# Low parts of ten weight slices: subtracted on GpSimd instead of VectorE

## The chip, the cores and the metric

The kernel runs on one core of a Trainium2 chip. The metric is the device time of one execution in microseconds (us), as the median of several runs. A core has TensorE (PE in the rows: matrix products), VectorE (DVE) and ScalarE (ACT) for work along rows, GpSimd (POOL) for the same kind of work, and SyncE (SP), which here issues all transfers. Each engine takes its instructions in the order in which they stand in its own queue; waits between engines are semaphores.

## The reference

```python
def _attn_ref(q, k, v, s):                 # q, k, v: (4, 8, 576, 64)
    scores = scale * np.matmul(q, k.transpose(0, 1, 3, 2))
    cum = np.cumsum(np.maximum(s, 0.0), axis=-1)
    bias = -(cum[:, :, :, None] - cum[:, :, None, :])
    scores = np.where(causal, -1000000000.0, scores + np.minimum(bias, 0.0))
    ...
    return np.matmul(attn, v)              # softmax over the last axis

def _moe_ref(x, w_in, w_out):              # first expert: 2304 x 512 -> 2048 -> 512
    h = x @ w_in
    g = h - np.tanh(h)
    return g @ w_out

def _moe2_ref(x, w_in, w_out):             # second expert, the same sizes
    h = x @ w_in
    g = h * np.clip(h + 3.0, 0.0, 6.0) / 6.0
    return g @ w_out
```

The attention's output is the first expert's input, and that expert's output is the second's. The weights of both experts come as 64-bit floats.

## The kernel before

**The three stages.** Attention runs to 185 us, the first expert from there to about 578 us, the second to the end. A matrix product is made to more than the engine's own precision by splitting both sides into a high part (rounded) and a low part (what is left), and by three passes: high by high, low weights by high, high weights by low.

**The first expert** goes through the 2304 tokens in five blocks, and in each block through 16 *slices* of 128 hidden features, numbered 0 to 15. A *step* is one slice of one block:

- three passes of 4 matmuls into a bank (`h{block}_{slice}_0` to `_2`, L903): high weights by high tokens, low weights by high tokens, high weights by low tokens. The first pass needs the slice's high weights, the second its low ones;
- on ScalarE tanh of the bank (L914), on VectorE bank minus tanh (L918), on ScalarE the high part of the result (L922), and its low part (L924), on VectorE in the first three blocks and on GpSimd in the last two. All four use one buffer, `g`, so the next step's tanh waits for L924;
- three passes of 4 matmuls for the output (`o{block}_{slice}_0` to `_2`, L934).

**The weights of a slice** are converted once, on the way into block 0, and stay in SBUF as `w{slice}` (128 partitions x 2048, high and low, for both matrices). Slices 0 to 5 are converted half by half (512 columns) during attention. Slices 6 to 15 (the diff's `range(6, 16)`) are converted whole (1024 columns) while block 0 already runs: one transfer of the raw words (L821), the absolute value on ScalarE (L825), four integer and clamp steps on VectorE (L826, L828, L830, L832) that make a 32-bit float from the two raw words, the high part on ScalarE (L851), and the low part as a subtraction (L852). The float stands in a work buffer from L825 to the end of L852: `wy` and `wy_b` take turns, and late in the block `wy_c` is there as well.

**Who sets the order.** The kernel does not write its instructions in a fixed order. Every piece is entered as an operation with an engine, a duration, what it comes after, its buffers and a priority. `Plan.schedule` then plays the whole program through with these durations and writes each engine's queue in the order of the planned starts. An operation entered with `port=True` is not planned beside another of that kind; the conversion's steps on VectorE are entered so. Durations given to the plan decide the order alone, and the chip takes what it takes.

After the first expert's weights VectorE and ScalarE convert those of the second (L987, L1017, L1018), which go out to HBM and come back as pieces in the last stage.

Of the kernel before, what the change touches and what calls it, by code (L numbers as in the profile page):

```python
# [66 lines left out]
]  # L67
UMX = ((0, 1, 2, 3, 4, 5), (4, 0, 1, 3, 2))
KDMA = ()
TINY, HUGE = (float(np.array([b], np.uint32).view(np.float32)[0]) for b in (0x38000000, 0x47F00000))  # L70

BLOCKS = [(0, t0, w) for t0, w in ((0, 512), (512, 512), (1024, 256), (1280, 512), (1792, 512))]
# [182 lines left out]
def vec_us(n, ghz, fixed):  # L255
    return (n / ghz + fixed) / 1e3
# [3 lines left out]
def kernel(  # L260
# [10 lines left out]
    nc = tc.nc  # L271
    plan = Plan()
    ctx.enter_context(tc.manual_schedule())

    def f32(a):
        return a.bitcast(F32)
# [39 lines left out]
    def r(b):  # L316
        return late[b.t] if isinstance(b.t, str) else b.t
# [132 lines left out]
    def heads(p):  # L450
# [10 lines left out]
        for i, a in enumerate(parts):  # L461
# [33 lines left out]
            oq1.append(plan.op("ACT", act + 0.22 * (p > 0), q1, [lq, al], [b1, tq], early(t + PRIO["q1"], 1), name=f"q1_{p}"))  # L495
            if p in KDMA:
                okh.append(plan.op("ACT", act, lambda a=a: nc.scalar.activation(r(b1)[1][0:64, a, 0:S], r(tq)[64:128, a], AF.Copy), [lk, al], [b1, tq], t + PRIO["kh"], name=f"kh{p}"))
# [314 lines left out]
    def rounded(src, n, prio, after, raws, words, name):  # L812

        raw, y = Buf(raws), Buf(words)

        def word(i):
            return r(raw).rearrange("p (n t) -> p n t", t=2)[:, :, i]

        def load():
            dst = r(raw) if src.ndim == 2 else r(raw).rearrange("p (l m) -> p l m", l=2)  # L820
            nc.sync.dma_start(dst, src)  # L821

        one, two, act = vec_us(n * 512, 1.92, 150), vec_us(n * 512, 0.96, 155), vec_us(n * 512, 1.2, 195)
        ld = plan.dma(load, 512 * n, after, [raw], prio, name=name)
        a = plan.op("ACT", act + 0.05, lambda: nc.scalar.activation(f32(r(y)), f32(word(1)), AF.Abs), [ld], [raw, y], prio)  # L825
        b = plan.op("DVE", one, lambda: nc.vector.tensor_scalar(  # L826
            f32(r(y)), f32(r(y)), TINY, HUGE, op0=ALU.max, op1=ALU.min), [a], [y], prio, port=True)
        b = plan.op("DVE", one, lambda: nc.vector.tensor_scalar(  # L828
            r(y), r(y), 3, 0x3FFFFFF8, op0=ALU.logical_shift_left, op1=ALU.bitwise_and), [b], [y], prio, port=True)
        b = plan.op("DVE", two, lambda: nc.vector.scalar_tensor_tensor(  # L830
            out=r(y), in0=word(1), scalar=-0x40000000, in1=r(y), op0=ALU.bitwise_and, op1=ALU.bitwise_or), [b], [raw, y], prio, port=True)
        b = plan.op("DVE", two, lambda: nc.vector.scalar_tensor_tensor(  # L832
            out=r(y), in0=word(0), scalar=29, in1=r(y), op0=ALU.logical_shift_right, op1=ALU.bitwise_or), [b], [raw, y], prio, port=True)
        return y, b

    def convert(fc, parts, prio, after, raws, words, there=()):
        n = len(parts)
        src = w1[fc][:, parts[0] * 512 : (parts[-1] + 1) * 512].bitcast(I32)
        y, b = rounded(src, n, prio, after, raws, words, f"wl{fc}_{parts[0]}")

        def hi():
            return slots[fc][:, parts[0] : parts[-1] + 1, 0:512]

        def lo():
            return slots[fc][:, parts[0] : parts[-1] + 1, 512:1024]

        def flat():
            return f32(r(y)).rearrange("p (i n) -> p i n", i=n)

        two, act = vec_us(n * 512, 0.96, 155), vec_us(n * 512, 1.2, 195)  # L850
        c = plan.op("ACT", act, lambda: nc.scalar.activation(hi(), flat(), AF.Copy), [b, *there], [y], prio)  # L851
        d = plan.op("DVE", two, lambda: nc.vector.tensor_sub(lo(), flat(), f32(hi())), [c], [y], prio, name=f"wd{fc}_{parts[0]}", port=True)  # L852
        return c, d

    wready, early, first_late, last_slots = {}, [], [], close
    for fc in range(NW):
        for part in range(2):
            wready[fc, part] = convert(
                fc, [part], PRIO["conv"] + 2 * fc + part, [st_done[1][0]], rawp, wyp)
            early += wready[fc, part]  # L860
    to_gg = change(early, "gg", [P, 4, 512], F32R, "B", None, ["gh0", "gh1", "gl0", "gl1"])
    plan.op("V", 0.0, lambda: None, early, hook=lambda: wywp.free.append(wy_t[:, 0:2].rearrange("p i n -> p (i n)")))
    for fc in range(NW, NFC):
        if fc == NFC - 2:
            last_slots = plan.op("V", 0.0, lambda: [slot_alloc(spaces[0], i, f"W{i}") for i in (NFC - 2, NFC - 1)], first_late, prio=0)
        beside = fc in LATE_D
        done = convert(fc, [0, 1], 5000 + 2 * fc, [st_done[20][0]], rdp if beside else rp, wywp, [last_slots])
        wready[fc, 0] = wready[fc, 1] = done
        first_late += done if beside else []
# [565 lines left out]
```

## Time and profile before

| | us |
|---|---|
| runs | 948.28, 948.75, 952.16 (median 948.75) |
| the profiled execution's own time | 947.19 |
| its span (first to last instruction) | 945.4 |
| TensorE busy | 931.6 |
| VectorE busy | 662.9 |
| ScalarE busy | 467.7 |
| GpSimd busy | 159.2 |

The profile is of one execution. The 1.8 us between its span and its own time lie around the program. An engine's busy time is a sum over the whole span; which engine is waited for in a stage is read from the idle time of the others in that stage. The granted clock of TensorE was 0.999 over the span (of its level of 2.4 GHz).

### The profile page before, as it was taken

What the parts mean: (1) busy time and instruction counts of PE and PEld (TensorE: products, weight loads), DVE (VectorE), ACT (ScalarE), POOL (GpSimd) and SP (SyncE); (2) the same over time, 40 slices, a digit from 0 to 9 for tenths busy, and PEclk for the clock granted to TensorE, in tenths of its full rate; (3) what the DMA queues carried; (4) which work ended last, traced back from release to release, by engine and by line L of the source; (5) the groups of instructions that cost most, each with busy time, mean ns of one, the idle gap of its engine ahead of it and who ended that gap; (6) DMA issues with size and microseconds to landing.
All of it is one profiled execution on the core that took longest, in us unless ns stands there. A gap on an engine that the chain in (4) does not pass through costs nothing.

```text
span 945.4 us, 18016 instructions
## 1 busy us (share of the span) xinstructions
PE 931.6 (99%) x7124; PEld 839.5 (89%) x7124; DVE 662.9 (70%) x1059; ACT 467.7 (49%) x720; POOL 159.2 (17%) x113
## 2 busy tenths in 40 slices
PE   8999999999999999999999999999999999999998
PEld 5888888788788889988888888999999999999997
DVE  7898887699985776676577641847767477674853
ACT  7678777555443444444344333544445445454441
POOL 7446656400000000022332321000000000000000
PEclk9999999999999999999999999999999999999999
DMA  5757785977235455563546862767887778776772
GB/s 142 185 153 204 200 227 144 247 308 218 96 121 223 179 183 218 200 202 156 219 149 224 262 215 85 258 214 221 274 268 242 215 226 270 269 245 209 220 217 89
DMA packets 69792, 193.74 MB, mean 205 GB/s; under 512 B 11856, under 2 KB 20656, under 8 KB 68428
## 3 DMA queue, kind: packets, MB, share of 16 engines
q1 hardware_dynamic: 69708, 192.59, 64.0%
q8 instruction: 56, 0.92, 0.4%
q14 instruction: 28, 0.23, 0.1%
HBM read 143.74 MB, written 44.09 MB: 199 GB/s over the span
## 4 chain that ended last, share of the span: by engine, by line
PE 88%; DVE 5%; DMA 3%; SPq 1%; issue 1%; ACT 1%; POOL 0%; DVEq 0%; POOLq 0%; ACTq 0%
PE bank L903 19%; PE pair L1271 19%; PE pair L1195 18%; PE bank L934 18%; PE bank L633 6%; PE bank L666 4%; PE bank L677 2%; PE bank L531 2%; PE wide L531 1%; DMA tq<-in_q_dram 1%; DMA raw_a<-in_w_dram 1%; SPq L735 1%; DMA w<-wdram 1%; DMA rb<-rdram 1%; DVE gg L924 0%
## 5 line engine op out<-in xcount | busy, mean ns | idle before, releaser
L934 PE MATMUL bank<-gg,w 128*128 128x512 f32 (+1 forms) x960 | 233.0, 368 | 1.4 <-ACT gg L922 1.4
L903 PE MATMUL bank<-xx,w 128*128 128x512 f32 (+1 forms) x960 | 232.4, 368 | 0.1
L934 PEld LDWEIGHTS bank<-gg,w 128*128 128x128 f32 x960 | 170.4, 188 | 31.5 <-ACT gg L922 1.8
L903 PEld LDWEIGHTS bank<-xx,w 128*128 128x128 f32 x960 | 170.3, 189 | 30.7 <-DVE xx L887 0.8
L1195 PE MATMUL pair<-op_w,w 128*128 128x384 f32 x648 | 118.0, 335 | 0.2 <-DVE g L918 0.2
L1195 PEld LDWEIGHTS pair<-op_w,w 128*128 128x128 f32 x648 | 112.4, 188 | 1.2 <-DVE g L918 0.6
L914 ACT ACTIVATE g<-bank 128x512 f32<-128x512 f32 (+1 forms) x80 | 44.5, 556 | 129.2 <-PE bank L903 57.3
L924 POOL TENSOR_TENSOR gg<-g,gg 128x512 fp32r<-128x512 f32 x32 | 48.0, 1501 | 345.4 <-ACT gg L922 248.2
L918 DVE TENSOR_TENSOR g<-bank,g 128x512 f32<-128x512 f32 (+1 forms) x80 | 50.8, 634 | 69.9 <-ACT g L914 68.9
L1271 PE MATMUL pair<-w,op_W 128*128 128x256 f32 x774 | 97.9, 283 | 1.2 <-DMA w<-wdram 1.2
L1271 PEld LDWEIGHTS pair<-w,op_W 128*128 128x128 f32 x774 | 95.4, 192 | 1.4 <-DMA w<-wdram 1.4
L922 ACT ACTIVATE gg<-g 128x512 fp32r<-128x512 f32 (+1 forms) x80 | 47.0, 588 | 51.3 <-DVE g L918 27.2
L633 PE MATMUL bank<-Q,K 128*128 128x320 f32 (+9 forms) x384 | 65.2, 309 | 0.4 <-DMA Q<-mdram 0.4
L636 ACT ACTIVATE pt<-bank 128x512 f32<-128x512 f32 (+2 forms) x128 | 58.9, 507 | 11.9 <-PE bank L633 9.9
L1271 PE MATMUL pair<-w,op_B 128*128 128x256 f32 x486 | 62.7, 283 | 0.0
L633 PEld LDWEIGHTS bank<-Q,K 128*128 128x128 f32 (+3 forms) x384 | 56.3, 184 | 5.5 <-issue 1.6
L1271 PEld LDWEIGHTS pair<-w,op_B 128*128 128x128 f32 x486 | 60.5, 192 | 0.0
L540 DVE CUSTOM_DVE_ANT_0 xr<-bank,xr 128x512 bf16<-128x512 f32 (+3 forms) x96 | 48.7, 508 | 15.3 <-PE bank L531 8.8
L474 POOL TENSOR_TENSOR Q<-tq,Q 64x1152 fp32r<-64x1152 f32 (+1 forms) x17 | 43.0, 2531 | 44.7 <-DVE xr L576 18.4
L666 PE MATMUL bank<-pt,vf 128*32 128x192 f32 (+3 forms) x1152 | 47.5, 316 | 1.3 <-ACT pt L636 1.3
L484 POOL TENSOR_TENSOR K<-tq,K 64x1152 fp32r<-64x1152 f32 (+1 forms) x17 | 42.9, 2525 | 9.6 <-ACT pt L636 5.2
L666 PEld LDWEIGHTS bank<-pt,vf 128*32 128x32 f32 x1152 | 32.4, 110 | 12.5 <-ACT pt L636 2.3
(322 smaller groups left out, 1349.7 us busy)
## 6 DMA issues: line engine op xcount, KB each, us to landing
w<-wdram SPq DMA_DIRECT2D x149, 512.0 KB
wdram<-cv SPq DMA_DIRECT2D x56, 512.0 KB
raw_c<-in_w_dram SPq DMA_DIRECT2D x11, 1024.0 KB
raw_b<-in_w_dram SPq DMA_DIRECT2D x11, 1024.0 KB
raw_a<-in_w_dram SPq DMA_DIRECT2D x12, 512.0 KB
vf<-in_v_dram SPq DMA_DIRECT2D x16, 330.0 KB
rb<-rdram SPq DMA_DIRECT2D x32, 144.0 KB
xdram<-xb SPq DMA_DIRECT2D x16, 288.0 KB
```

What stands on the lines that cost most here:

```text
L540: nc.vector.tensor_tensor_reduce(out=junk[0:rr, 0:w], in0=r(b)[0:rr, col : col + w], in1=maskB[:, 0:w] if hh < 0 else maskA[0:rr, m0 : m0 ...
L633: nc.tensor.matmul(o, w, x, start=(i == 0), stop=(i == len(mms) - 1), skip_group_check=True)
L636: nc.scalar.activation(r(pt), r(b)[:, 0 : CW[c]], AF.Exp, scale=0.125)
L666: nc.tensor.matmul(r((wide_b, rest_b)[far])[32 * i : 32 * i + 32, oc : oc + n], r(vf)[:, j, hh, d0 : d0 + 32], r(pts[hh][c])[:, col : col ...
L903: nc.tensor.matmul(r(ps)[:, 0:w], wt[:, c, :], x(c)[:, 0:w], start=(part == 0 and c == 0), stop=(part == 2 and c == NCC - 1),)
L914: nc.scalar.activation(r(g)[:, 0:w], r(ps)[:, 0:w], AF.Tanh)
L918: nc.vector.tensor_sub(x, r(ps)[:, 0:w], x)
L922: gho = plan.op("ACT", vec_us(w, 1.2, 205), lambda: nc.scalar.activation(r(gh)[:, 0:w], r(g)[:, 0:w], AF.Copy), [m, to_gg], [g, gh], base)
L924: glo = plan.op("DVE" if beside else "POOL", vec_us(w, 0.96, 155) if beside else vec_us(w, 0.44, 160), lambda: (nc.vector if beside else n ...
L934: nc.tensor.matmul(r(acc[e])[:, 0:w], a[:, es], bb[:, 0:w], start=f, stop=l)
L1195: nc.tensor.matmul(bank(k)[:, l], w[hw][:, l, kc], r(x)[:, hx, kc], start=(i in (1, 5, 2) and j == 0 and kc == 0), stop=(j == 2 and kc == ...
L1271: nc.tensor.matmul(r(c[k])[:, m * 256 : (m + 1) * 256], r(x)[:, hx, l, m * P : (m + 1) * P], w[hw][:, l], start=(i == order[chain_first[k] ...
```

## The change

For slices 6 to 15 the subtraction that makes the low part is entered as an operation of GpSimd, without `port=True`, and with a planned duration for GpSimd. Nothing else is edited.

```diff
+LO_POOL = range(6, 16)
...
         c = plan.op("ACT", act, lambda: nc.scalar.activation(hi(), flat(), AF.Copy), [b, *there], [y], prio)
-        d = plan.op("DVE", two, lambda: nc.vector.tensor_sub(lo(), flat(), f32(hi())), [c], [y], prio, name=f"wd{fc}_{parts[0]}", port=True)
+        if fc in LO_POOL:
+            d = plan.op("POOL", vec_us(n * 512, 0.44, 160), lambda: nc.gpsimd.tensor_sub(lo(), flat(), f32(hi())), [c], [y], prio, name=f"wd{fc}_{parts[0]}")
+        else:
+            d = plan.op("DVE", two, lambda: nc.vector.tensor_sub(lo(), flat(), f32(hi())), [c], [y], prio, name=f"wd{fc}_{parts[0]}", port=True)
         return c, d
```

Since the plan plays the program through with the new durations, the queues of all engines change their order from block 0 on. Lines behind the edit stand 4 further down in the changed kernel: L903, L918, L924 and L934 of before are L907, L922, L928 and L938 there, and L826 to L832 are L827 to L833.

GpSimd's queue at the start of the first expert, before: behind attention's last products (L743) and a constant stands the first L924 of the fourth block.

```order
L743 TENSOR_TENSOR xb0_83<-xb0_83,rb_85 128x576 x4
L784 MEMSET half_2714 128x1
L924 TENSOR_TENSOR gg_2792<-g0_78,gg_2792 128x512 x32
```

The same place in the changed kernel (`w6` to `w15` are the slices' weights, `wy_80`, `wy_b` and `wy_c` the work buffers):

```order
L785 MEMSET half_2714 128x1
L854 TENSOR_TENSOR w6_2703<-wy_b_2790,w6_2703 128x2x512
L854 TENSOR_TENSOR w7_2704<-wy_80,w7_2704 128x2x512
L854 TENSOR_TENSOR w8_2705<-wy_b_2790,w8_2705 128x2x512
L854 TENSOR_TENSOR w9_2706<-wy_80,w9_2706 128x2x512
L854 TENSOR_TENSOR w10_2707<-wy_b_2790,w10_2707 128x2x512
L854 TENSOR_TENSOR w11_2708<-wy_80,w11_2708 128x2x512
L854 TENSOR_TENSOR w12_2709<-wy_b_2790,w12_2709 128x2x512
L854 TENSOR_TENSOR w13_2710<-wy_80,w13_2710 128x2x512
L854 TENSOR_TENSOR w14_3102<-wy_b_2790,w14_3102 128x2x512
L854 TENSOR_TENSOR w15_3103<-wy_c_3144,w15_3103 128x2x512
```

Ten subtractions have come in, and nothing else of GpSimd's is moved.

VectorE's queue around slices 10 and 11, before (`wy_b` holds slice 10, then 12; `wy_80` holds slice 11):

```order
L832 SCALAR_TENSOR_TENSOR wy_b_2790<-raw_c_2713,wy_b_2790 128x1024
L743 TENSOR_TENSOR xb1_84<-xb1_84,rb_85 128x576
L924 TENSOR_TENSOR gg_2792<-g0_78,gg_2792 128x512
L852 TENSOR_TENSOR w10_2707<-wy_b_2790,w10_2707 128x2x512
L918 TENSOR_TENSOR g0_78<-bank4_72,g0_78 128x512
L826 TENSOR_SCALAR wy_80<-wy_80 128x1024
L826 TENSOR_SCALAR wy_b_2790<-wy_b_2790 128x1024
L924 TENSOR_TENSOR gg_2792<-g0_78,gg_2792 128x512
L828 TENSOR_SCALAR wy_80<-wy_80 128x1024
```

The same place in the changed kernel:

```order
L833 SCALAR_TENSOR_TENSOR wy_b_2790<-raw_c_2713,wy_b_2790 128x1024
L922 TENSOR_TENSOR g0_78<-bank1_66,g0_78 128x512
L827 TENSOR_SCALAR wy_80<-wy_80 128x1024
L829 TENSOR_SCALAR wy_80<-wy_80 128x1024
L831 SCALAR_TENSOR_TENSOR wy_80<-raw_d14_2711,wy_80 128x1024
L928 TENSOR_TENSOR gg_2792<-g0_78,gg_2792 128x512
L833 SCALAR_TENSOR_TENSOR wy_80<-raw_d14_2711,wy_80 128x1024
L922 TENSOR_TENSOR g0_78<-bank3_71,g0_78 128x512
L827 TENSOR_SCALAR wy_b_2790<-wy_b_2790 128x1024
```

The subtraction of slice 10 is gone from between the steps, and the four steps of slice 11 have moved up to where it stood; between the last step of a slice and the first of the next stands one L922.

TensorE's queue at the last slice of block 0, before (`w13`, `w14`, `w15` are the weights of these slices; a row of L903 with x4 is one pass, x8 two; four rows of L934 are one output pass):

```order
L903 MATMUL bank7_2318<-xx_2491,w14_3132 128x512 x4
L934 MATMUL bank2_70<-gg_2792,w13_2710 128x512
L934 MATMUL bank5_73<-gg_2792,w13_2710 128x512
L934 MATMUL bank0_65<-gg_2792,w13_2710 128x512
L934 MATMUL bank6_2317<-gg_2792,w13_2710 128x512
L934 MATMUL bank2_70<-gg_2792,w13_2710 128x512
L934 MATMUL bank5_73<-gg_2792,w13_2710 128x512
L934 MATMUL bank0_65<-gg_2792,w13_2710 128x512
L934 MATMUL bank6_2317<-gg_2792,w13_2710 128x512
L903 MATMUL bank1_66<-xx_2491,w15_3133 128x512 x8
```

The same place in the changed kernel:

```order
L938 MATMUL bank2_70<-gg_2792,w12_2709 128x512
L938 MATMUL bank5_73<-gg_2792,w12_2709 128x512
L938 MATMUL bank0_65<-gg_2792,w12_2709 128x512
L938 MATMUL bank6_2317<-gg_2792,w12_2709 128x512
L907 MATMUL bank1_66<-xx_2491,w15_3103 128x512 x4
L938 MATMUL bank2_70<-gg_2792,w13_2710 128x512
L938 MATMUL bank5_73<-gg_2792,w13_2710 128x512
L938 MATMUL bank0_65<-gg_2792,w13_2710 128x512
L938 MATMUL bank6_2317<-gg_2792,w13_2710 128x512
L907 MATMUL bank1_66<-xx_2491,w15_3103 128x512 x4
```

The second pass of slice 15, the one that needs its low part, stood behind all three output passes of slice 13; now it stands behind the first of them alone, with the other two behind it.

## Rows read from the trace of the kernel before

**Rows 1.** Page, part 1: busy us (share of span) xinstructions.

```profile
span 945.4 us, 18016 instructions
PE 931.6 (99%) x7124; PEld 839.5 (89%) x7124; DVE 662.9 (70%) x1059; ACT 467.7 (49%) x720; POOL 159.2 (17%) x113
```

**Rows 2.** TensorE's waits: engine, line, waited for: us, times, longest.

```profile
PE bank L934 <- ACT gg L922: 1.4, 1, 1.4
...
PE pair L1271 <- DMA w<-wdram: 1.2, 1, 1.2
...
PE pair L1195 <- DVE g L918: 0.2, 1, 0.2
```

**Rows 3.** Stages: length; PE, PEld, DVE, ACT, POOL busy; clock, DMA share, GB/s.

```profile
203.10:265.90 62.80, 61.38 (x271) 50.52 (x270) 60.03 (x76) 32.59 (x41) 0.00 (x0) 1.00 0.48 158
265.90:578.00 312.10, 311.95 (x1557) 265.87 (x1557) 208.15 (x304) 129.73 (x218) 47.04 (x32) 1.00 0.55 192
```

**Rows 4.** VectorE's groups, 203.1 to 265.9 us: busy us, mean ns | idle before.

```profile
L918 DVE TENSOR_TENSOR g<-bank,g 128x512 f32<-128x512 f32 x12 | 8.2, 684 | 0.1
...
L852 DVE TENSOR_TENSOR w<-wy_b,w 128x1024 fp32r<-128x1024 f32 x4 | 4.9, 1224 | 0.0
```

**Rows 5.** VectorE's timeline: start us, us, instruction [idle before].

```profile
203.13 1.23 DVE L852 TENSOR_TENSOR w<-wy_b,w 128x1024 fp32r<-128x1024 f32 x1
204.28 0.69 DVE L828 TENSOR_SCALAR wy<-wy 128x1024 int32<-128x1024 int32 x1
...
264.68 1.22 DVE L852 TENSOR_TENSOR w<-wy,w 128x1024 fp32r<-128x1024 f32 x1 [1.13 <-ACT w L851]
```

**Rows 6.** TensorE's timeline: its wait in block 0, and slice 15.

```profile
252.66 2.11 PE L934 MATMUL bank<-gg,w 128*128 128x512 f32 x8 [1.42 <-ACT gg L922]
...
264.60 1.98 PE L934 MATMUL bank<-gg,w 128*128 128x512 f32 x8
266.41 1.98 PE L903 MATMUL bank<-xx,w 128*128 128x512 f32 x8
268.23 1.07 PE L934 MATMUL bank<-gg,w 128*128 128x512 f32 x4
```

**Rows 7.** GpSimd's timeline: two subtractions of other lengths.

```profile
42.03 2.65 POOL L474 TENSOR_TENSOR Q<-tq,Q 64x1152 fp32r<-64x1152 f32 x1 [4.86 <-DVE xr L576]
...
438.20 1.29 POOL L924 TENSOR_TENSOR gg<-g,gg 128x512 fp32r<-128x512 f32 x1 [4.15 <-PE bank L934]
```

**Rows 8.** Timelines of VectorE and GpSimd where their instructions meet.

```profile
44.76 2.65 POOL L484 TENSOR_TENSOR K<-tq,K 64x1152 fp32r<-64x1152 f32 x1
45.21 0.56 DVE L540 CUSTOM_DVE_ANT_0 xr<-wide,xr 128x384 bf16<-128x384 f32 x1
45.80 2.22 DVE L477 CAST K<-tq 64x1152 fp32r<-64x1152 f32 x1
109.26 0.76 DVE L477 CAST K<-tq 64x1152 fp32r<-64x1152 f32 x1
...
415.48 1.21 DVE L832 SCALAR_TENSOR_TENSOR wy_b<-raw_c,wy_b 128x1024 int32<-128x1024 int32 x1
416.44 1.41 POOL L924 TENSOR_TENSOR gg<-g,gg 128x512 fp32r<-128x512 f32 x1 [2.30 <-ACT gg L922]
416.62 1.79 DVE L1018 TENSOR_TENSOR cv<-wy,cv 128x512 fp32r<-128x512 f32 x1
418.33 0.68 DVE L1018 TENSOR_TENSOR cv<-wy_b,cv 128x512 fp32r<-128x512 f32 x1
...
519.80 1.90 POOL L924 TENSOR_TENSOR gg<-g,gg 128x512 fp32r<-128x512 f32 x1 [4.14 <-PE bank L934]
520.62 1.63 DVE L826 TENSOR_SCALAR wy_b<-wy_b 128x1024 f32<-128x1024 f32 x1
523.38 0.68 DVE L828 TENSOR_SCALAR wy_b<-wy_b 128x1024 int32<-128x1024 int32 x1
```

## The prediction

> **What bounds the kernel now.** I read the page's busy times first. TensorE is busy for 931.6 of 945.4 us [rows 1], so a change elsewhere can gain only where TensorE waits, and can lose wherever it makes TensorE wait. The next view is therefore TensorE's waits. Behind attention there are three [rows 2]: 1.4 us on ScalarE's high part of a step, 1.2 us on a transfer in the last stage, 0.2 us on VectorE. The first ends at 252.66 us [rows 6], in block 0, among the conversions that the change touches. That 1.4 us is all that this stage has to give.
>
> Then the stage itself. Between the first and the last low part that the change moves (203.1 to 265.9 us) VectorE is busy for 60.0 of 62.8 us and GpSimd for none [rows 3]. So VectorE sets the pace of the conversions, and TensorE, which needs each slice as it comes, runs just behind. How close it runs is read at slice 15. Its low part starts at 264.68 us and takes 1.22, so it is there at 265.90 [rows 5]. TensorE begins the two first passes of that slice at 266.41, 8 matmuls that make room for the next row after 1.82 us [rows 6]; the second, which needs the low part, starts half of that later, at 267.32. The margin is 1.4 us. After this stage VectorE is busy for 208 of 312 us, but TensorE for 311.95 of 312.10 [rows 3]: what TensorE loses in block 0 cannot be made good later, and what VectorE is late by does not last.
>
> **What the change takes from VectorE.** Ten subtractions of 1.22 us [rows 4]. In a full queue one makes room for the next instruction 1.15 us after its start (203.13 to 204.28, [rows 5]), so 10 x 1.15 = 11.5 us leave VectorE's queue.
>
> **What it puts on GpSimd.** No row has a GpSimd subtraction of 1024 columns, but there are rows on both sides: 512 columns take 1.29 us and 1152 columns 2.65 [rows 7]. On the line between them 1024 columns take 1.29 + 512 x 1.36 / 640 = 2.38 us. GpSimd has nothing else to do there, so 10 x 2.38 us would fit. What decides is whether the two engines can work at the same time.
>
> **They cannot, for this kind of instruction.** At 45.80 us VectorE starts a cast that takes 0.76 us elsewhere; GpSimd's subtraction is under way since 44.76 and ends at 47.41, and the cast takes 2.22 us, until 48.02 [rows 8]: it got its turn when GpSimd was done. At 416.44 the reverse comes first. GpSimd's 512 columns are issued while VectorE's L832 runs until 416.69; they end at 417.85, 1.16 us after that. VectorE's next instruction, a subtraction of two SBUF tiles that takes 0.68 us by itself, takes 1.79 and ends at 418.41, 0.56 us after GpSimd. At 520.62 the clamp L826 does the same: GpSimd is at work until 521.70, and L826 takes 1.63 us, against 0.68 for a step of its length. In these rows one engine works at a time, for a whole instruction. VectorE's instruction that reads a PSUM bank passes: L540 at 45.21 takes 0.56 us in the middle of GpSimd's [rows 8].
>
> So of VectorE's instructions in the stage, the four conversion steps and L924 (L928 then) have to wait for a GpSimd subtraction, and L918 (L922) alone may pass, if a PSUM reader of another kind tells for it. The Trainium skill has a rule on this that speaks against the change ("SBUF — State Buffer", section "Who interferes with whom"): a VectorE instruction with two SBUF inputs, or one in a mode with two ports, and a GpSimd instruction that reads SBUF shut each other out, and whoever issues first keeps the port for its whole instruction. By that rule L918, with one SBUF input, would always pass; by the rows I count that only in the lower bound, 7.2 us below. The trace agrees with the rule wherever the two meet in [rows 8].
>
> **The sum in the conversions' queue.** A subtraction that has waited for its turn holds VectorE up by less than 2.38 us, since its start is already over: 1.16 against 1.29 us for 512 columns [rows 7, 8]. I take 2.38 - 0.13 = 2.25 us each, 22.5 us for ten. The queue thus gets 22.5 - 11.5 = 11.0 us longer. Of this some is hidden:
> - VectorE stands idle for 62.80 - 60.03 = 2.8 us in the stage [rows 3]. At best all of it lies under GpSimd's work.
> - The 12 L918 (8.2 us busy, [rows 4]), at some 0.6 us of the queue each, could pass under GpSimd's work: at most 7.2 us. The order says that few do. After the last step of a slice, GpSimd can only start when ScalarE has made the high part. By then VectorE, going on with its queue, has done the one L922 that stands behind that step, and the three conversion steps of the next slice that follow are held up by GpSimd, as behind slice 10.
>
> From both sides: all of it hidden gives 11.0 - 2.8 - 7.2 = 1.0 us, nothing hidden 11.0. I take the idle time as hidden and L918 as not, which is what the order of the queues shows: slice 15's low part comes 11.0 - 2.8 = 8.2 us later, at about 274 us.
>
> **From there to the end.** TensorE's queue is changed too. Before, the second pass of slice 15 stood behind all output passes of slice 13; now two of these stand behind it. Each is 4 matmuls, 0.91 us (half of the 1.82 us in [rows 6]). So 1.8 us more of work is left when the low part comes. Against that stands the margin of 1.4 us. The present wait of 1.4 us is no term of its own: TensorE's total wait follows from where the last slice lets it go on. The time grows by 8.2 + 1.8 - 1.4 = 8.6 us. No other stage adds: in the second and third block a few passes of TensorE's queue change places by one, with VectorE no longer full; from the fourth on its queue is the same as before.
>
> Against the profiled execution's own time, 947.19 us (span 945.4 and 1.8 around it), this gives 955.8 us. The median of the runs shown, 948.75, is 1.6 above that execution, and with it the sum is 957.4. I say **957 us**.
>
> **The rivals.**
> *The engines do work side by side there, and VectorE is relieved.* Then the queue is 11.5 us shorter, all slices are early, and that wait of 1.4 us goes: 948.75 - 1.4 = 947.3. For it speaks that VectorE is full and GpSimd empty [rows 3]. Against it speak all three meetings in [rows 8]. The point from which it decides: each subtraction would have to hold VectorE up by at most (11.5 + 2.8 + 1.4 - 1.8) / 10 = 1.4 us, where I have 2.25.
> *They shut each other out, but most of it is hidden.* If L918 and the idle time are hidden to the full, the growth is 1.0 + 1.8 - 1.4 = 1.4 us, 950 us; half of the L918 hidden gives 8.6 - 3.6 = 5.0 us, 954. For it: 12 L918 are in the stage. Against it: their place in the queue.
> *The work buffers add to it.* A buffer is free for the next-but-one slice when GpSimd is done, no longer VectorE. ScalarE's absolute value of that slice waits for this, with the tanh of the next step queued behind it. Where VectorE then has nothing that is ready, it idles again instead of filling up: without the 2.8 us hidden and with as much once more lost, the growth is 8.6 + 2.8 + 2.8 = 14.2 us, 963 us. For it: the chain from a slice's last step to the same buffer's next clamp is now one GpSimd subtraction long where it was 1.15 us. Against it: the other buffer's four steps lie in between.
> That the change doesn't do what it says can't be: the ten rows stand in GpSimd's queue.
>
> **How the numbers follow.** Relieved: 0.06. Mostly hidden, up to 4.7 us of growth: 0.16. The forecast, growth of 4.7 to 12 us: 0.66. Buffers, above that: 0.12. 0.5% of 948.75 is 4.7 us, about what a measurement of this kernel can tell from no change: faster than that is only conceivable through an order that I have not seen the good of, 0.02; slower 0.78; the rest, 0.20, the same. The range of 8 in 10 reaches from half-way into the hidden case, 951, to the price of the buffers' case, 963; it leaves out the relieved case (0.06) and half of each of these two (0.08 and 0.06).
>
> **What the profile would show.** Right: ten L854 on GpSimd of 2.3 us and up to 3.5 where they waited; conversion steps on VectorE with single durations up to 3 us beside their 0.68 and 1.22; slice 15's low part ready near 274 us; new waits of TensorE in block 0, on ScalarE's high parts and GpSimd's low parts of slices from about 9 on, 8 to 12 us in all; TensorE busy as before. Wrong: L827 to L833 at their old durations while L854 runs; or slice 15 ready before 268 us; or TensorE's waits in block 0 at 1.4 us or none, with the time lost in another stage.

## The result and the profile after

The changed kernel takes 962.31 us (median of 6 runs, 956.54 to 964.45), the kernel before 948.51 us beside it. The ratio is 1.0134, with a 95% interval from 1.0094 to 1.0173: it is slower by 13.8 us. The profiled execution took 964.45 us with a span of 962.7.

The page of the changed kernel, part 1:

```profile
span 962.7 us, 18022 instructions
...
PE 941.9 (98%) x7124; PEld 842.9 (88%) x7124; DVE 671.9 (70%) x1049; ACT 466.6 (48%) x720; POOL 183.9 (19%) x123
```

VectorE has ten instructions fewer than in [rows 1] and is busy for 9 us *more*. That is the first sign that its remaining instructions have become longer.

TensorE's timeline of the changed kernel: a wait in attention, the start of the first expert, slice 15's second pass, and the start of the second expert. Columns: start, duration, instruction, and in brackets the wait ahead of it:

```profile
37.88 0.38 PE L634 MATMUL bank<-Q,K 68*128 68x256 f32 x1 [0.80 <-DMA Q<-mdram]
...
191.21 3.08 PE L907 MATMUL bank<-xx,w 128*128 128x512 f32 x10
...
282.79 1.20 PE L907 MATMUL bank<-xx,w 128*128 128x512 f32 x4 [0.37 <-POOL w L854]
...
594.32 1.85 PE L1199 MATMUL pair<-op_w,w 128*128 128x384 f32 x9 [0.15 <-DVE g L922]
```

In the kernel before the same two stages begin with these rows:

```profile
185.19 3.04 PE L903 MATMUL bank<-xx,w 128*128 128x512 f32 x10
...
576.90 1.33 PE L1195 MATMUL pair<-op_w,w 128*128 128x384 f32 x6 [0.15 <-DVE g L918]
```

This cuts the 17.3 us between the two spans into three pieces:

| | before | after | difference |
|---|---|---|---|
| attention, to the first expert's first product | 185.2 | 191.2 | +6.0 |
| first expert, to the second expert's first product | 391.7 | 403.1 | +11.4 |
| the rest | 368.5 | 368.4 | -0.1 |

The 11.4 us are the subject here. Two groups of the windows of the changed kernel (length; PE, PEld, DVE, ACT, POOL busy; clock, DMA share, GB/s), the first in attention, the second from the first to the last subtraction on GpSimd:

```profile
36.00:48.00 12.00, 11.20 (x51) 9.82 (x49) 7.30 (x30) 7.16 (x12) 4.78 (x3) 0.59 0.49 106
209.25:282.74 73.49, 65.60 (x269) 48.71 (x267) 68.30 (x67) 32.15 (x42) 25.23 (x10) 1.00 0.41 142
```

The first row is where attention loses most of the 6.0 us: behind TensorE's wait at 37.88 the granted clock is 0.59 for 12 us, so part of that time at the lower of its two levels, and in the 12 us after that 0.84; in the kernel before it is 1.00 in both stretches. No instruction of the edit stands there, and up to the first expert VectorE, ScalarE and GpSimd have the same instructions in the same order in all the profiles here. Among the runs of the kernel before beside the first four experiments there are some with a mean clock of 0.999 (spans of 943.7 to 945.3 us) and some with 0.993 (950.7 and 951.9); the two runs of the changed kernel with a clock of 0.999 have spans of 956.1 and 954.8. The profiles of the kernels below enter the first expert anywhere from 183.9 to 195.6 us. So I compare the first expert's own length from here on.

The second row answers to the first of [rows 3]: the stage takes 73.49 us in place of 62.80. TensorE's waits in the first expert (us in total, times, longest):

```profile
PE bank L907 <- POOL w L854: 3.6, 8, 0.6
PE bank L907 <- ACT w L852: 3.5, 7, 1.2
...
PE bank L938 <- ACT gg L926: 0.7, 1, 0.7
```

Where [rows 2] had one wait of 1.4 us, there are now sixteen, 7.8 us, for the high and low parts of slices as they come. GpSimd's and VectorE's timelines show why:

```profile
209.25 2.40 POOL L854 TENSOR_TENSOR w<-wy_b,w 128x1024 fp32r<-128x1024 f32 x1 [17.72 <-ACT w L852]
...
233.52 2.39 POOL L854 TENSOR_TENSOR w<-wy,w 128x1024 fp32r<-128x1024 f32 x1 [7.27 <-ACT w L852]
...
280.34 2.40 POOL L854 TENSOR_TENSOR w<-wy_c,w 128x1024 fp32r<-128x1024 f32 x1 [6.13 <-ACT w L852]
```

```profile
209.31 2.89 DVE L829 TENSOR_SCALAR wy<-wy 128x1024 int32<-128x1024 int32 x1
212.24 1.23 DVE L831 SCALAR_TENSOR_TENSOR wy<-raw_d,wy 128x1024 int32<-128x1024 int32 x1
...
217.16 2.64 DVE L928 TENSOR_TENSOR gg<-g,gg 128x512 fp32r<-128x512 f32 x1 [0.16 <-ACT gg L926]
...
233.59 3.40 DVE L831 SCALAR_TENSOR_TENSOR wy_b<-raw_c,wy_b 128x1024 int32<-128x1024 int32 x1
...
272.80 1.96 DVE L827 TENSOR_SCALAR wy_c<-wy_c 128x1024 f32<-128x1024 f32 x1 [1.56 <-ACT wy_c L826]
...
280.79 0.69 DVE L922 TENSOR_TENSOR g<-bank,g 128x512 f32<-128x512 f32 x1 [1.01 <-ACT g L918]
282.24 1.05 DVE L928 TENSOR_TENSOR gg<-g,gg 128x512 fp32r<-128x512 f32 x1 [0.76 <-ACT gg L926]
```

L829 (0.69 us elsewhere) is issued 0.06 us behind GpSimd's subtraction and ends 0.55 us after it; L831 (1.23 by itself, at 212.24) takes 3.40 beside the next row of GpSimd. Each subtraction catches one step of VectorE, be it L827, L829, L831 or L928. The L922 at 280.79, which reads a PSUM bank, starts beside the last subtraction and keeps its 0.69 us; the L928 behind it is the one that is caught there.

### The profile page after: what moved, and what is told of

It reads as the page before. It is cut to its first block, busy times and chain, and to the rows that moved or that the text cites. A ratio compares the mean times of both kernels' runs of the same rounds, so it can differ in the third digit from the quotient of the medians.

```text
span 962.7 us, 18022 instructions
## 1 busy us (share of the span) xinstructions
PE 941.9 (98%) x7124; PEld 842.9 (88%) x7124; DVE 671.9 (70%) x1049; ACT 466.6 (48%) x720; POOL 183.9 (19%) x123
## 4 chain that ended last, share of the span: by engine, by line
PE 69%; DVE 1%; DMA 1%; ACT 0%; POOL 0%; issue 0%; POOLq 0%
PE pair L1275 18%; PE pair L1199 18%; PE bank L938 16%; PE bank L907 16%; DMA w<-wdram 1%; POOL gg L928 0%; DVE ev L959 0%; DVE f_D L1219 0%; DVE f_D L1210 0%; DVE f_D L991 0%; DVE f_E L1294 0%; ACT f_C L1218 0%; DVE f_w L1210 0%; DVE g L922 0%; ACT g L918 0%
## 5 line engine op out<-in xcount | busy, mean ns | idle before, releaser
L907 PE MATMUL bank<-xx,w 128*128 128x512 f32 (+1 forms) x960 | 235.4, 370 | 7.3 <-POOL w L854 3.6
L938 PE MATMUL bank<-gg,w 128*128 128x512 f32 (+1 forms) x960 | 234.3, 368 | 0.7 <-ACT gg L926 0.7
L907 PEld LDWEIGHTS bank<-xx,w 128*128 128x128 f32 x960 | 168.9, 188 | 43.8 <-POOL w L854 7.1
L938 PEld LDWEIGHTS bank<-gg,w 128*128 128x128 f32 x960 | 170.4, 189 | 31.1 <-ACT gg L926 1.2
L918 ACT ACTIVATE g<-bank 128x512 f32<-128x512 f32 (+1 forms) x80 | 44.5, 556 | 144.4 <-POOL gg L928 55.3
L928 POOL TENSOR_TENSOR gg<-g,gg 128x512 fp32r<-128x512 f32 x32 | 46.8, 1462 | 266.9 <-ACT gg L926 170.0
L922 DVE TENSOR_TENSOR g<-bank,g 128x512 f32<-128x512 f32 (+1 forms) x80 | 50.7, 634 | 61.1 <-ACT g L918 60.3
L634 PE MATMUL bank<-Q,K 128*128 128x320 f32 (+9 forms) x384 | 69.1, 321 | 0.9 <-DMA Q<-mdram 0.8
L637 ACT ACTIVATE pt<-bank 128x512 f32<-128x512 f32 (+2 forms) x128 | 59.9, 508 | 17.3 <-PE bank L634 14.7
L634 PEld LDWEIGHTS bank<-Q,K 128*128 128x128 f32 (+3 forms) x384 | 59.7, 194 | 6.5 <-issue 2.0
L928 DVE TENSOR_TENSOR gg<-g,gg 128x512 fp32r<-128x512 f32 (+1 forms) x48 | 32.8, 684 | 17.5 <-PE bank L938 10.1
```

Of the source, the lines that this page charges most:

```text
L634: nc.tensor.matmul(o, w, x, start=(i == 0), stop=(i == len(mms) - 1), skip_group_check=True)
L637: nc.scalar.activation(r(pt), r(b)[:, 0 : CW[c]], AF.Exp, scale=0.125)
L907: nc.tensor.matmul(r(ps)[:, 0:w], wt[:, c, :], x(c)[:, 0:w], start=(part == 0 and c == 0), stop=(part == 2 and c == NCC - 1),)
L918: nc.scalar.activation(r(g)[:, 0:w], r(ps)[:, 0:w], AF.Tanh)
L922: nc.vector.tensor_sub(x, r(ps)[:, 0:w], x)
L928: glo = plan.op("DVE" if beside else "POOL", vec_us(w, 0.96, 155) if beside else vec_us(w, 0.44, 160), lambda: (nc.vector if beside else n ...
```

## The experiments

Each changes the kernel before or the changed one at the place shown. "First expert" is the length defined above, 391.7 us before and 403.1 changed; each is read from one profiled execution. The time behind the first expert lies between 367.1 and 369.1 us in these profiles, so a difference of about 1 us in one row is no more than a hint. The whole time is a median, its ratio that to the kernel before on the same chip.

| | first expert | whole, us | ratio, 95% interval |
|---|---|---|---|
| e1 order of before, subtraction on GpSimd | 399.9 | 956.14 | 1.0074, 1.0047 to 1.0101 |
| e2 order of the change, subtraction on VectorE | 392.4 | 949.61 | 1.0003, 0.9980 to 1.0025 |
| e3 plan told to keep the two apart | 400.3 | 958.63 | 1.0093, 1.0058 to 1.0127 |
| e5 half of each | 394.6 | 952.53 | 1.0025, 1.0000 to 1.0051 |
| e7 slices 6 to 10 | 397.2 | 956.50 | 1.0070, 1.0045 to 1.0095 |
| e10 slices 11 to 15 | 396.1 | 952.74 | 1.0059, 1.0036 to 1.0082 |
| e6 zeros, at once | 399.5 | 954.85 | 1.0056, 1.0034 to 1.0078 |
| e8 zeros, behind the high part | 390.1 | 947.06 | 0.9980, 0.9959 to 1.0002 |
| e9 zeros by ScalarE | 390.0 | 947.69 | 0.9976, 0.9957 to 0.9995 |
| e11 one operand read | 390.0 | 945.94 | 0.9976, 0.9958 to 0.9993 |
| e13 two operands, at once | 393.5 | 949.01 | 1.0012, 0.9991 to 1.0032 |
| e12 the clamp on GpSimd instead | 397.8 | 954.31 | 1.0068, 1.0044 to 1.0092 |

**Order or engine: e1, e2, e3.** The edit does two things: it takes another engine, and the plan writes other queues. In e1 the plan's entry is that of before, and the ten are executed on GpSimd:

```diff
-d = plan.op("DVE", two, lambda: nc.vector.tensor_sub(lo(), flat(), f32(hi())), [c], [y], prio, ..., port=True)
+sub = (nc.gpsimd if fc in range(6, 16) else nc.vector).tensor_sub
+d = plan.op("DVE", two, lambda: sub(lo(), flat(), f32(hi())), [c], [y], prio, ..., port=True)
```

> All queues stand in the order of the kernel before; only the engine of the ten subtractions is GpSimd. Theory (the two engines shut each other out): the conversion steps behind each subtraction are stretched as in the changed kernel, slice 15's low part is 8 to 11 us late, TensorE's order keeps its margin of 1.4 us and does not have the 1.8 us of moved output passes: the first expert takes 398 to 401 us (391.7 before, 403.1 changed), the whole 954 to 957 us. Rival (the new order of the queues costs the time): without the new order at most 2 us stay, first expert below 394 us, whole 947 to 950 us. Rival (an attention that is slower because of the change): attention ends near 191 us again; by chance alone: near 185 us, or at a lower granted clock also in the kernel before.

In e2 the entry is that of the changed kernel, and VectorE executes:

```diff
-    d = plan.op("POOL", vec_us(n * 512, 0.44, 160), lambda: nc.gpsimd.tensor_sub(...
+    d = plan.op("POOL", vec_us(n * 512, 0.44, 160), lambda: nc.vector.tensor_sub(...
```

> All queues stand in the order of the changed kernel, with the ten subtractions executed by VectorE at the places that the plan gave to GpSimd's. Theory (shutting out): ten subtractions of 1.15 us on VectorE in place of some 2.25 us of hold-up; what stays is the 1.8 us of output passes behind slice 15's second pass less the margin of 1.4 us, and a little waiting where the subtraction now stands ahead of VectorE's next step: first expert 392 to 395 us, whole 948 to 951 us. Rival (the order costs the time): first expert 400 to 403 us, whole 956 to 959 us.

In e3 `port=True` is added to the changed kernel's entry for GpSimd.

> The subtractions stay on GpSimd, but are entered with port=True, so that the plan puts no two-port step of VectorE beside them and writes the queues for that. Theory (shutting out): the time on the shared way is used whatever the plan knows; ten times 2.40 less 1.15 us are 12.5 us, less VectorE's idle time and what L922 can hide: first expert 397 to 402 us, whole 953 to 959 us. Rival (the plan's ignorance is what costs): with it told, first expert 390 to 394 us, whole 946 to 950 us.

The engine costs 8.2 us with no change of order (e1), the order 0.7 us with no change of engine (e2). The sum is 8.9; the other 2.5 of the 11.4 us come only with both. The row of e1 in which slice 15's low part is made, and its waits of TensorE in this stage (line numbers there are one higher than before for L903, L922 and L934):

```profile
274.01 2.38 POOL L853 TENSOR_TENSOR w<-wy,w 128x1024 fp32r<-128x1024 f32 x1 [5.91 <-ACT w L851]
```

```profile
PE bank L935 <- ACT gg L923: 4.1, 2, 3.5
PE bank L904 <- POOL w L853: 1.8, 3, 0.9
...
PE bank L904 <- ACT w L851: 0.5, 1, 0.5
```

It is there at 276.39, 90.2 us behind the first expert's start at 186.24; before it was 265.90 - 185.19 = 80.7. So it is 9.4 us late, the margin takes 1.4 of it, which leaves 8.0; the first expert grows by 8.2. In e2 VectorE's rows have their old durations in the new order:

```profile
205.99 1.23 DVE L854 TENSOR_TENSOR w<-wy_b,w 128x1024 fp32r<-128x1024 f32 x1
207.14 0.69 DVE L829 TENSOR_SCALAR wy<-wy 128x1024 int32<-128x1024 int32 x1
```

There slice 15's low part is ready at 268.29, 80.3 us behind the first expert's start at 188.02 and so 0.4 us earlier than before: the moved passes find it in time. The stage of e2, in the columns of [rows 3]:

```profile
205.99:268.29 62.30, 60.87 (x266) 49.31 (x265) 60.23 (x76) 31.56 (x41) 0.00 (x0) 1.00 0.47 159
```

Telling the plan (e3) helps little. The steps no longer start beside a subtraction in the plan, but on the chip some still do (an L928 at 254.01 takes 2.88 us), and VectorE's busy time shrinks only to leave it idle: 60.62 us busy in a stage of 71.50, 10.9 us idle.

```profile
202.70:274.20 71.50, 63.47 (x272) 50.23 (x271) 60.62 (x66) 32.36 (x42) 25.86 (x10) 1.00 0.43 145
```

**How the cost adds up: e5, e7, e10.** In e5 the half for the first matrix stays on VectorE:

```diff
+v = plan.op("DVE", ..., lambda: nc.vector.tensor_sub(lo()[:, 0], flat()[:, 0], f32(hi()[:, 0])), ...)
+d = plan.op("POOL", ..., lambda: nc.gpsimd.tensor_sub(lo()[:, 1], flat()[:, 1], f32(hi()[:, 1])), ...)
```

> Each of the ten low parts is cut in two: the half for the first matrix (512 columns) stays on VectorE, the half for the second goes to GpSimd. Theory (shutting out): VectorE gets rid of some 0.55 us of queue a slice and is held up for about 1.16 us by a subtraction of 512 columns, 0.6 us a slice, about half of what the whole subtraction costs: first expert 394 to 399 us (391.7 before, 403.1 changed), whole 950 to 956 us. Rival (the low part is late because GpSimd is slow at it, and nothing else): the half that the first passes wait for is now made by VectorE in 0.69 us, and first expert is 390 to 393 us.

In e7 the changed kernel has `LO_POOL = range(6, 11)`, in e10 `range(11, 16)`.

> Only the low parts of slices 6 to 10 go to GpSimd, those of 11 to 15 stay on VectorE. Theory (the hold-ups add up in VectorE's queue, and what is lost early is not made good later): five times 1.1 us, up to 1.8 us for moved passes, less the margin of 1.4 us: first expert 395 to 399 us, whole 951 to 955 us. Rival (only the last slices matter, since GpSimd's part of the chain is longer there): first expert 390 to 393 us.

> Only the low parts of slices 11 to 15 go to GpSimd, those of 6 to 10 stay on VectorE: the other half of e7. Theory (every hold-up is lost for good, early or late): five times 1.1 us, as there: first expert 396 to 399 us, and with the 5.5 us of e7 about the 11.4 us of the whole change. Rival (the last slices cost more, since GpSimd's 2.40 us stand at the end of the chain in place of 1.22): 399 to 401 us. Rival (they cost less, because VectorE's idle time lies there): 392 to 395 us.

In the first expert all three fall where the theory has them (e7's whole time is 1.5 us above what was written): +2.9 us for half of each, +5.5 and +4.4 us for half of the slices. Early slices cost no less than late ones, and the two halves make 9.9 of the 11.4 us. So what VectorE loses in slices 6 to 10 is not made good by slice 15.

**What there was to win: e9.** ScalarE writes zeros in place of the low parts (low weights of slices 6 to 15 left out):

```diff
+d = plan.op("ACT", act, lambda: nc.scalar.activation(lo(), flat(), AF.Copy, scale=0.0), [c], [y], prio, ...)
```

> GpSimd stays empty, and ScalarE writes the low parts of slices 6 to 15 as zeros (these low weights are left out of the result). VectorE's queue is 11.5 us shorter, and nothing shuts it out. Theory: this is what there was to win: TensorE's wait in block 0 goes, first expert 390 to 392 us, whole 946 to 949 us. Rival (TensorE was held by more than VectorE in this stage, so there was more to win): below 389 us. Rival (the new order costs): 396 us or more. Reservation: ten more instructions of 1.1 us on ScalarE may hold up its tanh, and show as waits on ScalarE.

390.0 us, and no wait of TensorE in block 0 is left in its list. With VectorE relieved of the ten subtractions and nothing on GpSimd, the first expert gains 1.7 us.

**What shuts VectorE out: e6, e8, e11, e13.** These keep a GpSimd instruction at the subtraction's entry in the plan and change what it reads. In e6 it is `memset(f32(lo()), 0.0)`.

> In the order of the changed kernel GpSimd only writes the low parts of slices 6 to 15 (zeros, so these low weights are left out of the result) and reads no SBUF. Theory in its narrow form (a GpSimd instruction that reads SBUF is what shuts VectorE out): VectorE's steps beside it keep 0.68 and 1.22 us, its queue is 11.5 us shorter, TensorE's waits in block 0 go: first expert 390 to 392 us, whole 946 to 949 us. In its wide form (any GpSimd instruction on SBUF): the steps beside it are stretched until it ends, and the growth goes by its length, ten times the length less 1.15 us. Rival (the order costs the time): first expert 400 to 403 us whatever GpSimd does.

It came out in a way that neither theory had. The zeros depend on nothing, so eight of them ran in a row as soon as GpSimd was free, beside the casts with which block 0 starts (POOL, DVE and PE rows of e6):

```profile
187.15 7.18 POOL L854 MEMSET w<- 128x1024 f32 x8
```

```profile
187.28 7.66 DVE L891 CAST xx<-xr 128x512 fp32r<-128x512 f32 x2
```

```profile
194.66 9.60 PE L907 MATMUL bank<-xx,w 128*128 128x512 f32 x29 [7.03 <-DVE xx L891]
```

Two casts that take 0.75 us in the changed kernel take 7.66, and TensorE waits 7.03 us, most of the 7.8 that e6 loses. An instruction that reads no SBUF can shut out VectorE too, and VectorE did not get in between two of them. For the subtraction's place it says nothing, so e8 puts the zeros behind the high part, by writing the work buffer first:

```diff
+def fill():
+    nc.gpsimd.memset(f32(r(y)), 0.0)
+    nc.gpsimd.memset(f32(lo()), 0.0)
+    return nc.gpsimd.memset(f32(lo()[:, 0]), 0.0)
```

> In place of the subtraction GpSimd writes zeros, behind ScalarE's high part as the subtraction stood: the work buffer, the low part, and half of the low part again, about 2.4 us in all, with no SBUF operand read (low weights of slices 6 to 15 are left out of the result). It separates three things. If any GpSimd instruction on SBUF shuts out any of VectorE's with SBUF operands: all of L827 to L833 and L928 are stretched beside it, first expert 400 to 403 us. If a writer shuts out only the steps with one SBUF input (L827, L829) and lets those with two (L831, L833, L928) pass: L827 and L829 up to 3 us, the others at 1.22 and 0.68 us, first expert 394 to 400 us. If the lateness of the buffer is what costs: no step is stretched, and first expert is still over 396 us.

Two meetings in e8, GpSimd's rows and then VectorE's (L933 is the step's low part there, two SBUF inputs):

```profile
205.70 0.96 POOL L855 MEMSET wy_b<- 128x1024 f32 x1 [17.67 <-ACT w L852]
206.59 0.97 POOL L856 MEMSET w<- 128x1024 f32 x1
...
212.26 1.55 POOL L855 MEMSET wy<- 128x1024 f32 x1 [3.69 <-ACT w L852]
213.75 0.96 POOL L856 MEMSET w<- 128x1024 f32 x1
```

```profile
205.78 2.32 DVE L829 TENSOR_SCALAR wy<-wy 128x1024 int32<-128x1024 int32 x1
...
213.07 0.69 DVE L933 TENSOR_TENSOR gg<-g,gg 128x512 fp32r<-128x512 f32 x1 [0.16 <-ACT gg L931]
213.68 1.22 DVE L831 SCALAR_TENSOR_TENSOR wy_b<-raw_d,wy_b 128x1024 int32<-128x1024 int32 x1
```

L829, with one input, is held (2.32); L933 and L831, with two, run beside the writes at 0.69 and 1.22. It is the middle case of the three, with one correction: only five one-input steps are held, by 0.2 to 1.6 us, so the stage is as fast as with nothing on GpSimd (390.1), not 394 to 400.

e11 reads one operand, e13 two; neither needs the high part, so both start right behind the conversion's last step:

```diff
-lambda: nc.gpsimd.tensor_sub(lo(), flat(), f32(hi()))
+lambda: nc.gpsimd.tensor_scalar_mul(lo(), flat(), 0.0)
```

> GpSimd's instruction at the subtraction's place reads one operand, the work buffer, times zero, and writes the low part (low weights of slices 6 to 15 are left out of the result). It stands between the writer of e8 and the subtraction. If reading is what shuts out VectorE's steps with two SBUF inputs: L831, L833 or L928 are stretched beside it until it ends, and first expert grows by its length, some 10 times its length less 1.15 us, as far as VectorE meets it. If only a GpSimd instruction that is as long as the subtraction does it, or its second input: the two-input steps keep 1.22 and 0.68 us, and first expert is 390 to 392 us as in e8.

```diff
-lambda: nc.gpsimd.tensor_sub(lo(), flat(), f32(hi()))
+lambda: nc.gpsimd.tensor_sub(lo(), flat(), flat())
```

> As the run with one input, with one difference: GpSimd subtracts the work buffer from itself, so it reads two SBUF operands (zeros as low parts of slices 6 to 15; these low weights are left out of the result) and starts, like that one, without waiting for ScalarE's high part. If the second operand is what shuts out VectorE's two-input steps: L831, L833 or L928 beside it take up to 3 us, first expert 396 to 402 us. If what mattered was the place behind ScalarE's high part: steps keep 0.68 and 1.22 us, and first expert stays at 390 us.

e11, GpSimd and then VectorE:

```profile
210.44 3.15 POOL L854 TENSOR_SCALAR w<-wy 128x1024 fp32r<-128x1024 f32 x1 [2.19 <-DVE wy L833]
```

```profile
211.47 0.93 DVE L829 TENSOR_SCALAR wy_b<-wy_b 128x1024 int32<-128x1024 int32 x1
212.33 0.68 DVE L928 TENSOR_TENSOR gg<-g,gg 128x512 fp32r<-128x512 f32 x1
212.93 1.22 DVE L831 SCALAR_TENSOR_TENSOR wy_b<-raw_d,wy_b 128x1024 int32<-128x1024 int32 x1
```

GpSimd is at work from 210.44 to 213.59. L829 (one input) is held for 0.24 us, and then L928 and L831 (two inputs) run inside at 0.68 and 1.22. A one-input step that starts later is held too:

```profile
255.10 2.77 POOL L854 TENSOR_SCALAR w<-wy_b 128x1024 fp32r<-128x1024 f32 x1 [2.72 <-DVE wy_b L833]
```

```profile
257.08 1.34 DVE L827 TENSOR_SCALAR wy_c<-wy_c 128x1024 f32<-128x1024 f32 x1 [1.53 <-ACT wy_c L826]
```

L827 ends at 258.42, 0.55 us behind GpSimd's end, as beside a subtraction. No two-input step of e11 starts in the first microsecond of GpSimd's instruction; e12, below, has some that do, and they are held. e13:

```profile
213.82 1.90 POOL L854 TENSOR_TENSOR w<-wy_b 128x1024 fp32r<-128x1024 f32 x1 [4.10 <-DVE wy_b L833]
222.00 1.90 POOL L854 TENSOR_TENSOR w<-wy 128x1024 fp32r<-128x1024 f32 x1 [6.28 <-DVE wy L833]
```

```profile
215.39 0.87 DVE L928 TENSOR_TENSOR gg<-g,gg 128x512 fp32r<-128x512 f32 x1 [1.14 <-ACT gg L926]
...
222.44 2.01 DVE L829 TENSOR_SCALAR wy_b<-wy_b 128x1024 int32<-128x1024 int32 x1
```

With two operands the same L928 and L829 are held until GpSimd is done (215.72 and 223.90) and end 0.54 and 0.55 us later. So the subtraction with two operands holds VectorE's one- and two-input steps until it ends, and the multiplication with one lets two-input steps in before its end. e13 differs from e11 in the operation too, not in the operand alone as its expectation says, and no run parts the two; when within its time GpSimd reads, no run shows either. The size was off, though: 393.5 us, not 396 to 402. The instruction is shorter than the subtraction of two tiles (1.90 for 2.40), and without the wait for the high part GpSimd starts while VectorE does the one L922 behind its last step; eight steps are held by 0.2 to 1.6 us, 9.3 us together, where the changed kernel's nine make 17.9.

**Another step for GpSimd: e12.** The kernel before, with the clamp of these slices on GpSimd, which has one input (in effect, for slices 6 to 15):

```diff
-b = plan.op("DVE", one, lambda: nc.vector.tensor_scalar(
+b = plan.op("POOL", 2.77, lambda: nc.gpsimd.tensor_scalar(
     f32(r(y)), f32(r(y)), TINY, HUGE, op0=ALU.max, op1=ALU.min), [a], [y], prio)
```

> The kernel before, with another step moved: the clamp (L826, one SBUF input) of slices 6 to 15 goes to GpSimd, and the subtractions stay on VectorE. It tries for a version that is faster than both. If a GpSimd instruction with one SBUF input lets VectorE's two-input steps pass and costs its one-input steps some 0.4 us each, as in the run with one input, VectorE's queue becomes 10 x 0.6 us shorter and up to 10 x 0.4 us longer: TensorE's wait of 1.4 us in block 0 goes, first expert 390 to 392 us (391.7 before), whole 1 to 2.5 us below the kernel before. If the clamp shuts out VectorE as the subtraction does (2.8 us each): first expert 400 us or more. If the chain of each slice, longer by 2.1 us, is what TensorE waits for: 393 to 396 us.

It is no improvement: 397.8 us. The clamp takes 3.6 to 4.6 us there, not 2.8, and VectorE waits for it (0.66, 0.34, 1.55, 0.94 and 0.94 us). A GpSimd row and two of VectorE's:

```profile
200.56 3.64 POOL L827 TENSOR_SCALAR wy<-wy 128x1024 f32<-128x1024 f32 x1 [1.18 <-ACT wy L825]
```

```profile
200.63 2.06 DVE L831 SCALAR_TENSOR_TENSOR wy_b<-raw_c,wy_b 128x1024 int32<-128x1024 int32 x1
...
225.87 0.69 DVE L829 TENSOR_SCALAR wy_b<-wy_b 128x1024 int32<-128x1024 int32 x1 [1.55 <-POOL wy_b L827]
```

L831 has two inputs and starts 0.07 us behind GpSimd: it is held (2.06 in place of 1.22), but ends 1.5 us before GpSimd does. So an instruction of GpSimd with one operand does hold up a two-input step that meets its start. For how long can be estimated: beside a subtraction a held L831 ends 1.08 us behind GpSimd (236.99 against 235.91), so here it was let go some 202.69 - 1.08 - 200.56 = 1.05 us after the clamp's start. The waits for the clamp, 4.4 us in all, are more than I had put on the longer chain; steps are held besides, and which of the two makes how much of the 6 us no run shows. No kernel of this study that computes the whole reference is faster than the one before.

## Why the prediction was right

**The bound.** VectorE full, TensorE just behind it, 1.4 us to win: e9 gave 1.7, e11 1.7, e8 1.6. In e8 and e9 no wait of TensorE is left in block 0, so there is no more to win there.

**Removed and added.** Ten subtractions left VectorE's queue, 11.5 us by the 1.15 us of each (e2's rows have the same 1.15, 205.99 to 207.14), though not all of their place was filled again, as shown below. GpSimd needs 2.40 us for 1024 columns, 2.38 estimated.

**Shutting out.** Right: that the engine and not the order costs is shown by e1 and e2. The Trainium skill's rule ("SBUF — State Buffer", section "Who interferes with whom") held in the subtraction's case and in e8: against a GpSimd instruction that only writes, it lets VectorE's two-input steps pass. It is too wide in one: it has a two-input step of VectorE shut out by any GpSimd instruction that reads SBUF, and beside e11's one-operand reader L928 took 0.68 us, though in e12 an L831 that met the start of one took 2.06. The measurement decides. The price was a little high: nine held steps add up to 17.9 us (2.0 each), and the tenth, L928 at 282.24, loses 0.4, where I had ten times 2.25. VectorE's busy time in the stage grew by 68.30 - 60.03 = 8.3 us; the prediction had 11.0. (Of the 8.3, 18.3 - 11.5 = 6.8 are the hold-ups less the subtractions; the rest is one L928 more in the stage and less overlap of neighbouring instructions.)

**Hidden work, the step that was mis-sized.** "At best all of it lies under GpSimd's work", I wrote of VectorE's idle 2.8 us, and took it so. It was not hidden but grew, to 73.49 - 68.30 = 5.2 us. So slice 15's low part was 282.74 - 191.21 - 80.71 = 10.8 us late, not 8.2. Two errors offset each other in part: the hold-ups were put 2.7 us too high, the idle time 5.2 us too low (2.8 taken off, 2.4 to be added).

By e2 and e11 the idle time comes with taking the subtractions out of this order, not with the shutting out. In the changed kernel's order VectorE is idle for 62.30 - 60.23 = 2.1 us with the subtractions on VectorE (e2), and for 61.02 - 55.52 = 5.5 us in e11, where the hold-ups add up to 4.4 us and not to 18.3:

```profile
205.05:266.07 61.02, 61.02 (x271) 50.54 (x270) 55.52 (x68) 33.12 (x43) 30.56 (x10) 1.00 0.50 170
```

```profile
217.53 0.69 DVE L928 TENSOR_TENSOR gg<-g,gg 128x512 fp32r<-128x512 f32 x1 [1.14 <-ACT gg L926]
...
264.44 0.69 DVE L922 TENSOR_TENSOR g<-bank,g 128x512 f32<-128x512 f32 x1 [1.01 <-ACT g L918]
265.89 0.69 DVE L928 TENSOR_TENSOR gg<-g,gg 128x512 fp32r<-128x512 f32 x1 [0.76 <-ACT gg L926]
```

With the 1.53 us ahead of L827 at 257.08, these are the changed kernel's waits of 1.14 (ahead of the L928 at 224.32), 1.56, 1.01 and 0.76 us, in the same places. At the first three, where VectorE waits for ScalarE, e2 has a subtraction to do. In e11 TensorE waits for none of this; in the changed kernel it adds to the hold-ups.

**L918 (L922) not under GpSimd's work** was right but for one: the L922 at 280.79, behind the last conversion step, passed under GpSimd's work. e13 shows the reason: take away the wait for the high part, and the instruction that passes lies under GpSimd again.

**From there to the end.** 10.8 late, plus 1.8 for the moved passes, less the margin of 1.4, makes 11.2; measured 11.4. In e1, without moved passes, 9.4 - 1.4 = 8.0; measured 8.2. In e2, with moved passes and a low part that is 0.4 us early, 1.8 - 1.4 - 0.4 = 0.0; measured 0.7. By this sum 3.2 us come only with both changes (2.5 measured): the 1.8 of the moved passes, which cost when the part is late, and the 1.4 by which it is later than in e1. "No other stage adds" held for everything behind the first expert (368.4 against 368.5 us).

**The rivals.** Side by side fell with the first L829. Mostly hidden fell with the idle time. The work buffers: this rival's amount of idle time came near (2.8 + 2.8 in it, 5.2 measured), its cause did not act. ScalarE did wait for GpSimd's subtraction before two absolute values, but these were done at 212.83 and 258.23, and VectorE came to their clamps only at 215.12 and 263.58; the tanh behind each waited for an L928 of VectorE. The order came to 0.7 us by itself.

**What the profile would show.** Ten L854 of 2.39 to 2.88 us (2.3 to 3.5 written), steps up to 3.40 (3 written), TensorE's waits 7.8 us (8 to 12 written). Slice 15's low part was ready at 282.74, or 276.7 counted from where the first expert began before (274 written). TensorE was not busy as before: 941.9 us for 931.6.

**The whole time.** 962.3 against 957 forecast: 2.8 us are the first expert's (11.4 for 8.6), the rest attention's clock by the profiles, which the sum had not, and which varies in the kernel before as well. The growth of 13.8 us is in the class of the buffers' rival (above 12), that of the first expert in the forecast's. The clock in attention, which is chance, brought the time to 0.7 us below the end of the range (963), and that the sum of the stage came within 2.8 us is in part luck, by the two errors that offset each other. e3, with the same ten subtractions on GpSimd, had a median of 958.63.

## What to carry to other kernels

An idle engine is not free if its instructions hold up those of the full one: before work is moved from VectorE to GpSimd, look in the trace for a place where both work at once and read whether one of them has become longer. Count what the moved instruction holds up (2.0 us here) against what it saves (1.15), and count it in full where the queue is full, early or late. Do not count on idle time to hide it: the place that a moved instruction leaves can itself stay empty (2.1 us idle with the subtractions, 5.2 without). Which instruction GpSimd executes matters: VectorE's two-input steps ran at their own speed beside its writes, and beside a one-operand multiplication once its first microsecond was over.

## What the runs showed of the hardware

- A GpSimd subtraction of two SBUF operands holds VectorE's steps until it ends: 2.89 for 0.69 us, 3.40 for 1.23. L922, which reads a PSUM bank, is not held (0.69 at 280.79).
- A GpSimd instruction with one operand lets VectorE in before its end: L829 at 211.47 ended 1.96 us after GpSimd's start and 1.2 us before its end, and two-input steps behind it ran at 0.68 and 1.22 us. But it holds a two-input step that meets its start (2.06 for 1.22, e12), and a one-input step late in it until it ends (1.34 for 0.69, at 257.08).
- Eight writes of 0.9 us in a row kept a pair of casts waiting for 7 us; VectorE did not get its turn between them.
- GpSimd's durations at 128x1024 differ by instruction: 0.96 us to write zeros, 1.90 to subtract a tile from itself, 2.40 for two tiles, 2.8 to 3.6 for one multiplication beside VectorE's work, 3.6 to 4.6 for a clamp.
- Attention, with the same work in all profiles, ended between 183.9 and 195.6 us. In the changed kernel's profile a wait of 0.80 us was followed by 12 us at a granted clock of 0.59.
